# Small vectors through GpSimd's queue, and another order of loads and row work in a kernel of pooled attention and a token-mixing MLP

## The chip, the cores and the metric

The kernel runs on one core of a Trainium2 chip. Its time is that of one launch, in microseconds on the device; the runs of a kernel are given with their median. The core has five engines that run their own instruction streams: TensorE (PE; its weight loads are counted apart as PEld), VectorE (DVE), ScalarE (ACT), GpSimd (POOL) and SyncE (SP), which here only issues transfers. Sixteen DMA engines carry the transfers of all queues.

## The reference

Eight batches, eight heads of 64, 576 tokens. The keys and values are averaged over groups of eight tokens, so each head has 72 of them. The attention's output is the input of one token-mixing MLP layer.

```python
k_p = k.reshape(B, H, 72, 8, D).mean(axis=3)
v_p = v.reshape(B, H, 72, 8, D).mean(axis=3)
scores = scale * np.matmul(q, k_p.transpose(0, 1, 3, 2))
attn = softmax(scores)
x = np.matmul(attn, v_p)          # as (B, 576, 512)
a1 = alpha1 * x + beta1
u = x + lam * np.einsum('ts,bsd->btd', w_tok, a1)
a2 = alpha2 * u + beta2
out = u + lam * (np.maximum(a2 @ w_ch1, 0.0) @ w_ch2)
```

## The kernel before, in words

**Tiles.** A batch's q and k come as two tiles `qk_raw` (four heads each, tokens 0 to 511, f32, 512 KB for q and 512 KB for k) and one small tile `rem_raw` (tokens 512 to 575, four transfers of 64 KB). v comes as two tiles `v_u`, each by two transfers: 64 groups and the last 8. The tiles of each kind have two buffers, so a new load waits until its buffer's readers are done.

**Attention of one batch.** GpSimd casts q to `q_bf` (L112) and sums k over four tokens into `k_bf` (L119, L120), and does the same for the remainder (L105, L106); batch 0 has VectorE or ScalarE do some of it. TensorE transposes q (`att_F`), finishes the pooling of k with a matrix of eighths (`att_K`, casts to `kpT` at L334), and VectorE sums v over eight tokens (`att_V`, L340 and L342, into `vp`). Then, head by head, `att_S` makes the scores and their exponentials (ScalarE, L354), `att_AV` the weighted sums with a column for the denominator, a reciprocal and a product on VectorE (L374, L376) into `x_tm`, and after every second head `att_X` scales two heads' columns into the bf16 tile `xs` (L383, the four full row tiles, and L387, the remainder).

**Mix and MLP.** `mix_T` multiplies `w_tok` with `xs` for one row tile (five matmuls of 512 columns, L417), adds `x` on VectorE (L419) and scales to `u_bf` (L421). `mix_uT` transposes `u_bf` into `u_fm`. The MLP takes blocks of four row tiles, 9 blocks for the 36 row tiles of all batches: sixteen first-layer tiles `mlp_A` (four matmuls of 512 columns, a ReLU on ScalarE at L446) and then sixteen second-layer parts `mlp_B` (four matmuls, L459; the last part of a row tile adds to `u` at L464, and the output transfer goes out at L466).

**What sets the order.** Nothing is scheduled by a tool. The front (L473 to L545) is written out: it does batch 0's attention and mix. For the blocks, `todo` holds pairs of a position and a step, and they are issued in order of the position: first-layer tiles at 0 to 15, second-layer parts at 16 to 31, the next batch's attention and mix among them (block n does batch n + 1), and the loads of the batch after that. Each engine runs its own instructions in the order in which they were issued. In block 0, batch 1's work stands later (`late`), since its loads come late. `keep_warm` gives TensorE matmuls on zeros that nobody reads.

**Queues.** SyncE issues all loads of q, k, v and all outputs; ScalarE's queue issues five loads of small vectors (alpha1, lam, alpha2, beta1, beta2) at the start; GpSimd's queue issues `w_tok` and the eight weight loads, which cast from f32 to bf16 on the way. SyncE's and ScalarE's transfers take eight completion semaphores in turn, so the ninth transfer waits until the first has landed, and so on. GpSimd's queue has eight of its own.

## Time and profile before

| | |
|---|---|
| median of 3 runs | 395.27 us (394.63 to 396.18) |
| the profiled execution | 391.7 us, span of its instructions 390.0 us |
| TensorE busy | 360.9 us (93% of the span) |
| VectorE, ScalarE, GpSimd busy | 226.3, 189.9 and 72.1 us |
| mean granted TensorE clock | 0.992 |
| bytes moved | 43.01 MB, 110 GB/s over the span |

The profile is one execution with the start and the duration of each instruction. A matmul's duration includes its way through the array, so four matmuls in a row take less than four durations; rows that stand for several (x4) give the time from the first start to the last end. What an engine waited for stands in brackets behind its row, with the idle time.

### The profile page before, as it was taken

The page shows a single profiled execution, that of the slowest core. Times are in us where ns is not written, and L with a number is a line of the kernel's source. Part 1 is how long each engine was busy: PE and PEld are TensorE (multiplying, and loading weights), DVE is VectorE, ACT ScalarE, POOL GpSimd, SP SyncE. Part 2 cuts the span into 40 slices and gives each one's busy share as a digit, 9 for nine tenths or more (in the row PEclk, how much of TensorE's full clock was granted, in tenths as well). Part 3 has the DMA queues.
Part 4 walks back from the last instruction along what each step waited for, and adds up shares of the span by engine and source line. Part 5 has one row for each costly group of instructions (what it writes and reads, how often), then busy time and mean ns, then how long its engine had stood idle before and what let it go on. Part 6 is the DMA issues. An engine that isn't in the chain of part 4 may idle for free.

```text
span 390.0 us, 5932 instructions
## 1 busy us (share of the span) xinstructions
PE 360.9 (93%) x2275; PEld 193.8 (50%) x2275; DVE 226.3 (58%) x469; ACT 189.9 (49%) x380; POOL 72.1 (18%) x86
## 2 busy tenths in 40 slices
PE   6579999699999999899989998999899999999994
PEld 2355555345554555355535553455455544544541
DVE  6677459875497549745875578637873685011011
ACT  3644666117831683168505860387038713822710
POOL 6272243420150015000510042003300000000000
PEclk9999999989999999999999999999999999999998
DMA  5999995903861187116811591139210011002011
GB/s 176 246 166 214 258 196 111 229 31 106 203 162 55 55 202 162 55 54 140 224 55 50 119 251 44 42 84 249 82 44 12 2 55 55 0 27 82 0 53 57
DMA packets 34705, 43.01 MB, mean 110 GB/s; under 512 B 2218, under 2 KB 24814, under 8 KB 34676
## 3 DMA queue, kind: packets, MB, share of 16 engines
q1 hardware_dynamic: 31744, 37.76, 37.7%
q0 software_dynamic: 2912, 4.86, 7.0%
q8 instruction: 18, 0.29, 0.3%
q14 instruction: 11, 0.09, 0.1%
q10 hardware_dynamic: 20, 0.01, 0.0%
HBM read 38.04 MB, written 9.44 MB: 122 GB/s over the span
## 4 chain that ended last, share of the span: by engine, by line
PE 73%; DVE 19%; DMA 4%; issue 1%; ACT 1%; SPq 1%; POOL 1%
PE ps_h L443 32%; PE ps_ch L459 21%; PE ps_tok L417 12%; DVE x_tm L376 5%; DVE xs L383 5%; DMA qk_raw<-in_k_dram 4%; DVE xs L387 3%; PE ps_uT L432 2%; PE ps_sc L352 2%; DVE rec L374 2%; DVE u_sb L464 2%; PE ps_q L298 1%; PE ps_av L368 1%; PE ps_warm L407 1%; DVE v_u L340 1%
## 5 line engine op out<-in xcount | busy, mean ns | idle before, releaser
L459 PE MATMUL ps_ch<-w,Hj 128*128 128x512 bf16 x576 | 141.4, 381 | 0.0
L443 PE MATMUL ps_h<-u_fm,w 128*128 128x512 bf16 x576 | 132.4, 379 | 0.0
L446 ACT ACTIVATE Hj<-ps_h,bias_cols 128x512 bf16<-128x512 f32 x144 | 99.1, 689 | 40.4 <-PE ps_h L443 39.3
L443 PEld LDWEIGHTS <-w 128*128 128x128 bf16 x576 | 62.9, 114 | 49.8 <-issue 0.3
L459 PEld LDWEIGHTS <-Hj 128*128 128x128 bf16 x576 | 54.6, 98 | 50.9 <-issue 2.2
L434 ACT COPY u_fm<-ps_uT 128x512 bf16<-128x512 bf16 x36 | 21.1, 586 | 101.2 <-PE ps_uT L432 101.0
L417 PE MATMUL ps_tok<-xs,wtT 128*128 128x512 bf16 (+1 forms) x200 | 50.7, 385 | 10.7 <-DVE xs L383 10.7
L354 ACT ACTIVATE ET<-ps_sc 72x288 f16<-72x288 f32 x128 | 44.8, 402 | 26.7 <-PE ps_sc L352 25.9
L464 DVE TENSOR_TENSOR u_sb<-u_sb,ps_ch 128x512 f32<-128x512 f32 x36 | 24.4, 681 | 50.3 <-PE ps_ch L459 50.2
L419 DVE TENSOR_TENSOR u_sb<-x_tm,ps_tok 128x512 f32<-128x512 f32 (+1 forms) x40 | 27.5, 687 | 35.4 <-PE ps_tok L417 35.1
L340 DVE TENSOR_TENSOR v_u<-v_u 72x512 f32<-72x512 f32 x64 | 36.4, 569 | 3.2 <-DMA v_u<-in_v_dram 1.7
L417 PEld LDWEIGHTS <-wtT 128*128 128x128 bf16 (+1 forms) x200 | 18.8, 99 | 35.0 <-DVE xs L383 13.9
L334 DVE CAST kpT<-ps_kp 64x144 bf16<-64x144 f32 x32 | 9.8, 305 | 43.1 <-PE ps_kp L330 42.9
L376 DVE TENSOR_TENSOR x_tm<-ps_av,rec 128x320 f32<-128x320 f32 x64 | 31.5, 492 | 2.2
L112 POOL CAST q_bf<-qk_raw 128x1024 bf16<-128x1024 f32 x14 | 14.9, 1065 | 87.0 <-DMA qk_raw<-in_q_dram 87.0
L352 PE MATMUL ps_sc<-qT,kpT 128*72 128x288 bf16 x128 | 28.3, 307 | 2.1 <-DVE x_tm L376 1.1
L421 DVE TENSOR_TENSOR u_bf<-u_sb,al_bc 128x512 bf16<-128x512 f32 (+1 forms) x38 | 26.7, 702 | 1.5
L119 POOL TENSOR_TENSOR qk_raw<-qk_raw 128x512 f32<-128x512 f32 x16 | 22.2, 1387 | 19.8 <-DMA qk_raw<-in_k_dram 16.8
L383 DVE TENSOR_TENSOR xs<-x_tm,lamal_bc 128x512 bf16<-128x512 f32 x31 | 25.1, 808 | 1.0
L368 PEld LDWEIGHTS <-ET 72*128 72x128 f16 x256 | 16.7, 102 | 17.5 <-DVE vp L342 2.5
L374 DVE RECIPROCAL rec<-ps_av 128x5 f32<-128x5 f32 x64 | 12.1, 189 | 17.4 <-PE ps_av L372 16.9
L368 PE MATMUL ps_av<-vp,ET 72*128 72x66 f16 x256 | 18.7, 199 | 3.6 <-DVE vp L342 3.6
(91 smaller groups left out, 236.6 us busy)
## 6 DMA issues: line engine op xcount, KB each, us to landing
qk_raw<-in_q_dram SPq DMA_DIRECT2D x16, 512.0 KB, 8.0
qk_raw<-in_k_dram SPq DMA_DIRECT2D x16, 512.0 KB, 7.6
v_u<-in_v_dram SPq DMA_DIRECT2D x16, 512.0 KB, 5.6
out_dram<-u_sb SPq DMA_DIRECT2D x32, 256.0 KB, 3.4
w<-in_moe_w_ch_dram POOLq DMA_DIRECT2D x8, 512.0 KB, 12.5
rem_raw<-in_q_dram SPq DMA_DIRECT2D x16, 64.0 KB
rem_raw<-in_k_dram SPq DMA_DIRECT2D x16, 64.0 KB, 2.3
v_u<-in_v_dram SPq DMA_DIRECT2D x16, 64.0 KB
```

The costliest lines, as they stand in the source:

```text
L340: nc.vector.tensor_tensor(out=t[:, :, 0:n], in0=t[:, :, 0:n], in1=t[:, :, n:2 * n], op=ALU.add)
L352: nc.tensor.matmul(out=ps_sc[0:SPG, 0:288], lhsT=kpT_pool[u][:, hh, r, :], rhs=st["qT"][u][:, S * r + n0:S * r + n0 + 288])
L354: nc.scalar.activation(out=ET[:, 64 + n0:64 + n0 + 288], in_=ps_sc[0:SPG, 0:288], func=AF.Exp, bias=0.0, scale=0.125)
L368: nc.tensor.matmul(out=av[:, c, :], lhsT=ET[:, m0:m0 + 128], rhs=vp1[:, hh, :])
L376: nc.vector.tensor_tensor(out=x[:, :, dd:dd + D], in0=av[:, :, 0:64], in1=rec.unsqueeze(2).to_broadcast((P, 5, D)), op=ALU.mult)
L383: eng.tensor_tensor(out=xs[:, 0:4, cols], in0=x[:, 0:4, cols], in1=lamal_bc[:, cols].unsqueeze(1).to_broadcast((P, 4, D * (h1 - h0))), op= ...
L417: nc.tensor.matmul(out=ps_tok, lhsT=wtT[0:kk, at, t0:t0 + P], rhs=xs[0:kk, sc, :], start=(sc == 0), stop=(sc == 4))
L419: nc.vector.tensor_tensor(out=s["u"][p0:p1, :], in0=st1[b]["x"][p0:p1, c, :], in1=ps_tok[p0:p1, 0:DM], op=ALU.add)
L443: nc.tensor.matmul(out=ps_h, lhsT=w1_of(cc, j), rhs=u_fm[n][:, cc, :], start=(cc == 0), stop=(cc == 3))
L446: nc.scalar.activation(out=t, in_=ps_h, func=AF.Relu, bias=bias_cols[:, j:j + 1], scale=1.0)
L459: nc.tensor.matmul(out=ps, lhsT=Hj[n, j][:, 128 * m:128 * m + 128], rhs=w2[j // 4][:, j % 4, :], start=(j == 0), stop=(j == NJ - 1))
L464: nc.vector.tensor_tensor(out=u, in0=u, in1=ps, op=ALU.add)
```

## The change

**Loads at the start.** The five small vectors go through GpSimd's queue, two ahead of its mask building and three behind it. On SyncE's queue the first v tile stands ahead of the remainder, and the v tile's small part behind it. `load_v` takes a list of the parts that it issues. beta1 times lam is multiplied straight into `xs`, where it went through a tile `lamb1` and two copies.

**The front.** The `kpT` casts of batch 0 are ScalarE's (`att_K` with `nc.scalar.copy`). The third broadcast (alpha2) and the transposed beta2 stand behind the first four heads' scores. Both v sums of the second half stand ahead of its scores. The scaling of two heads that GpSimd does stands earlier, the first row sum of `w_tok` behind the last weighted sums, and of the 13 matmuls of `keep_warm` 5 stay. The four mixes follow each other, and the first four first-layer tiles begin on three of the four row tiles (384 columns) before the last row tile is transposed; the last 128 columns follow.

**The blocks.** The q and k loads of the batch after the next move to positions 0.4 and 1.4, the remainder to 0.9, and v to 5.8 and 12.4 (before: remainder 3.5, v 4.6 and 11.2, q and k right behind each). `q_bf` and `k_bf` get a fourth buffer. Scores, weighted sums and mixes of batches 2 to 7 stand one position earlier. In block 0 the first two of four `att_X` are GpSimd's, and the four scalings of `w2` (L276) stand at 4.2 to 9.3, before at 5.0 to 14.0.

SyncE's queue at the start of the program, before. The names are the tile and the input tensor; `DMAHW0` to `DMAHW7` are the completion semaphores that an issue waits for.

```order
L77 DMA qk_raw<-in_q_dram 128x4x256
L77 DMA qk_raw<-in_k_dram 128x4x256
L87 DMA rem_raw<-in_q_dram 128x1x128 x2
L87 DMA rem_raw<-in_k_dram 128x1x128 [waits DMAHW0_49]
L87 DMA rem_raw<-in_k_dram 128x1x128 [waits DMAHW1_49]
L96 DMA v_u<-in_v_dram 64x4x512 [waits DMAHW3_49]
L96 DMA v_u<-in_v_dram 8x4x512 [waits DMAHW4_49]
L77 DMA qk_raw<-in_q_dram 128x4x256 [waits DMAHW5_49]
L77 DMA qk_raw<-in_k_dram 128x4x256 [waits DMAHW6_49]
```

The same place after:

```order
L77 DMA qk_raw<-in_q_dram 128x4x256
L77 DMA qk_raw<-in_k_dram 128x4x256
L99 DMA v_u<-in_v_dram 64x4x512
L87 DMA rem_raw<-in_q_dram 128x1x128 x2
L87 DMA rem_raw<-in_k_dram 128x1x128 x2
L99 DMA v_u<-in_v_dram 8x4x512
L77 DMA qk_raw<-in_q_dram 128x4x256 [waits DMAHW0_49]
L77 DMA qk_raw<-in_k_dram 128x4x256 [waits DMAHW1_49]
```

Eight transfers now stand ahead of the first wait, where four stood, and v's large part is the third.

VectorE in the front, from the last product of the first four heads to the sums of the second v tile, before:

```order
L376 TENSOR_TENSOR x_tm_252<-ps_av_280,rec_286 128x5x64
L334 CAST kpT_1_139<-ps_kp_316 64x144 x2
L383 TENSOR_TENSOR xs_0_157<-x_tm_252,lamal_bc_72 128x4x128
L387 TENSOR_TENSOR xs_0_157<-x_tm_252,lamal_bc_72 64x128
L383 TENSOR_TENSOR xs_0_157<-x_tm_252,lamal_bc_72 128x4x128
L387 TENSOR_TENSOR xs_0_157<-x_tm_252,lamal_bc_72 64x128
L340 TENSOR_TENSOR v_u_102<-v_u_102 72x2x256
L340 TENSOR_TENSOR v_u_102<-v_u_102 72x2x128
L342 TENSOR_TENSOR vp1_2_144<-v_u_102 72x2x64
```

The same place after:

```order
L380 TENSOR_TENSOR x_tm_249<-ps_av_277,rec_283 128x5x64
L387 TENSOR_TENSOR xs_0_155<-x_tm_249,lamal_bc_72 128x4x128
L391 TENSOR_TENSOR xs_0_155<-x_tm_249,lamal_bc_72 64x128
L387 TENSOR_TENSOR xs_0_155<-x_tm_249,lamal_bc_72 128x4x128
L391 TENSOR_TENSOR xs_0_155<-x_tm_249,lamal_bc_72 64x128
L344 TENSOR_TENSOR v_u_95<-v_u_95 72x2x256
L344 TENSOR_TENSOR v_u_95<-v_u_95 72x2x128
L346 TENSOR_TENSOR vp1_2_142<-v_u_95 72x2x64
```

The two casts of `kpT`, for which VectorE had to wait until the second k had been summed, no longer stand ahead of the slices and the v sums.

SyncE's queue from the last output of a block into the next block, before:

```order
L466 DMA out_0_dram<-u_sb_1089 128x512 [waits DMAHW4_49,DVE_49]
L87 DMA rem_raw_1669<-in_q_dram 128x1x128 [waits DMAHW5_49]
L87 DMA rem_raw_1669<-in_q_dram 128x1x128 [waits DMAHW6_49]
L87 DMA rem_raw_1669<-in_k_dram 128x1x128 [waits DMAHW7_49]
L87 DMA rem_raw_1669<-in_k_dram 128x1x128 [waits DMAHW0_49]
L96 DMA v_u_1681<-in_v_dram 64x4x512 [waits DMAHW1_49,DVE_49]
L96 DMA v_u_1681<-in_v_dram 8x4x512 [waits DMAHW2_49]
L77 DMA qk_raw_1684<-in_q_dram 128x4x256 [waits DMAHW3_49,Pool_49]
L77 DMA qk_raw_1684<-in_k_dram 128x4x256 [waits DMAHW4_49]
L96 DMA v_u_1770<-in_v_dram 64x4x512 [waits DMAHW5_49,DVE_49]
```

The same place after:

```order
L477 DMA out_0_dram<-u_sb_1091 128x512 [waits DMAHW7_49,DVE_49]
L77 DMA qk_raw_1640<-in_q_dram 128x4x256 [waits DMAHW0_49,Pool_49]
L77 DMA qk_raw_1640<-in_k_dram 128x4x256 [waits DMAHW1_49]
L87 DMA rem_raw_1643<-in_q_dram 128x1x128 [waits DMAHW2_49]
L87 DMA rem_raw_1643<-in_q_dram 128x1x128 [waits DMAHW3_49]
L87 DMA rem_raw_1643<-in_k_dram 128x1x128 [waits DMAHW4_49]
L87 DMA rem_raw_1643<-in_k_dram 128x1x128 [waits DMAHW5_49]
L77 DMA qk_raw_1655<-in_q_dram 128x4x256 [waits DMAHW6_49,Pool_49]
L77 DMA qk_raw_1655<-in_k_dram 128x4x256 [waits DMAHW7_49]
L99 DMA v_u_1720<-in_v_dram 64x4x512 [waits DMAHW0_49,DVE_49]
```

Both q, k pairs now stand right behind the output, and no v load, with its wait for VectorE, stands ahead of them.

The diff, cut to its core:

```diff
-        bf = work.tile([P, 4, 4, D], BF, tag="q_bf", bufs=3, name="q_bf")
+        bf = work.tile([P, 4, 4, D], BF, tag="q_bf", bufs=4, name="q_bf")
...
     load_qk(0, 0)
-    for i, src in ((1, moe_alpha1), (0, moe_lam), (2, moe_alpha2), (3, moe_beta1)):
-        n = 65 if i in (0, 3) else 1
-        nc.scalar.dma_start(out=vecs[0:n:64, i],
-                            in_=src.unsqueeze(0).to_broadcast((1 + n // 65, DM)))
-    nc.scalar.dma_start(out=b2row, in_=moe_beta2.rearrange("(c p) -> c p", p=P))
+    load_v(0, 0, (0,))
     load_rem(0)
-    load_v(0, 0)
+    load_v(0, 0, (1,))
     load_qk(0, 1)
     load_v(0, 1)
+    for i, src in ((1, moe_alpha1), (0, moe_lam)):
+        n = 65 if i in (0, 3) else 1
+        nc.gpsimd.dma_start(out=vecs[0:n:64, i],
+                            in_=src.unsqueeze(0).to_broadcast((1 + n // 65, DM)))
...
+    nc.gpsimd.dma_start(out=vecs[0:65:64, 3], in_=moe_beta1.unsqueeze(0).to_broadcast((2, DM)))
+    nc.gpsimd.dma_start(out=vecs[0:1, 2], in_=moe_alpha2.unsqueeze(0))
+    nc.gpsimd.dma_start(out=b2row, in_=moe_beta2.rearrange("(c p) -> c p", p=P))
...
-    def mlp_A(n, j):
-        ps_h = gp("ps_h")
+    def mlp_A(n, j, t0=0, t1=512):
+        if t0 == 0:
+            ps_A[j] = gp("ps_h")
+        ps_h = ps_A[j]
         for cc in range(4):
-            nc.tensor.matmul(out=ps_h, lhsT=w1_of(cc, j), rhs=u_fm[n][:, cc, :],
+            nc.tensor.matmul(out=ps_h[:, t0:t1], lhsT=w1_of(cc, j), rhs=u_fm[n][:, cc, t0:t1],
                              start=(cc == 0), stop=(cc == 3))
...
-    broadcast(2, al2_bc)
-    setup_vectors()
...
-    att_K(0, 0, nc.vector.tensor_copy)
+    att_K(0, 0, nc.scalar.copy)
     for h in range(4):
         att_S(0, h)
...
     att_V(0, 1)
+    broadcast(2, al2_bc)
+    setup_vectors()
     for h in range(4):
         att_AV(0, h)
...
-    att_K(0, 1, nc.vector.tensor_copy)
+    att_K(0, 1, nc.scalar.copy)
     att_X(0, 0, 2)
     att_X(0, 2, 4)
     att_V(0, 2)
+    att_V(0, 3)
     for h in (4, 5, 6):
         att_S(0, h)
-    att_V(0, 3)
...
     setup_wtok(0, nc.scalar.copy)
+    att_X(0, 4, 6, nc.gpsimd)
     setup_wtok(1, nc.scalar.copy)
-    keep_warm(3)
-    att_X(0, 4, 6, nc.gpsimd)
-    setup_rowsum(0)
     att_AV(0, 6)
     att_AV(0, 7)
+    setup_rowsum(0)
     setup_wtok(2, nc.scalar.copy)
     setup_rowsum(1)
-    keep_warm(3)
+    setup_wtok(3, nc.scalar.copy)
     att_X(0, 6, 8)
...
     mix_uT((0, 2))
-    keep_warm(2)
+    keep_warm(3)
+    mlp_A(0, 0, 0, 384)
     mix_uT((0, 3))
-    keep_warm(3)
+    for j in range(1, 4):
+        mlp_A(0, j, 0, 384)
+    for j in range(4):
+        mlp_A(0, j, 384, 512)
...
-            at = 17.0 + 0.9 * h if late else 14.1 + 1.0 * h
+            at = 17.0 + 0.9 * h if late else 13.1 + 1.0 * h
...
-                todo.append((at + lag + 0.1, lambda h=h: att_X(b, h - 1, h + 1)))
+                eng = nc.gpsimd if late and h < 5 else nc.vector
+                todo.append((at + lag + 0.1, lambda h=h, eng=eng: att_X(b, h - 1, h + 1, eng)))
         for c in range(5):
-            at = 26.2 + 0.9 * c if late else 26.0 + c
+            at = 26.2 + 0.9 * c if late else 25.0 + c
...
-                todo.append((5.0 + 3 * g, lambda g=g: scale_w2(g)))
+                todo.append((4.2 + 1.7 * g, lambda g=g: scale_w2(g)))
...
-                late = 17.0 if b == 1 else 0.0
-                todo.append((late + 3.5, lambda b=b: load_rem(b + 1)))
                 for u in range(2):
-                    at = 22.0 + 0.1 * u if b == 1 else 4.6 + 6.6 * u
+                    at = 20.0 + 0.2 * u if b == 1 else 0.4 + 1.0 * u
+                    todo.append((at, lambda b=b, u=u: load_qk(b + 1, u)))
+                    at = 22.0 + 0.2 * u if b == 1 else 5.8 + 6.6 * u
                     todo.append((at, lambda b=b, u=u: load_v(b + 1, u)))
-                    todo.append((at + 0.1, lambda b=b, u=u: load_qk(b + 1, u)))
+                todo.append((20.1 if b == 1 else 0.9, lambda b=b: load_rem(b + 1)))
```

More of the change, by code (lines that the diff above doesn't have):

```diff
@@ L90, in load_rem, with load_v @@
         st1[b]["rem_raw"] = raw
-    def load_v(b, u):
-        v_u = work.tile([SPG, 4, 8, D], FP, tag="v_u", bufs=2, name="v_u")
-        for g0, g1 in ((0, 64), (64, SPG)):
+    def load_v(b, u, parts=(0, 1)):
+        if parts[0] == 0:
+            st1[b]["v"][u] = work.tile([SPG, 4, 8, D], FP, tag="v_u", bufs=2, name="v_u")
+        v_u = st1[b]["v"][u]
+        for part in parts:
+            g0, g1 = ((0, 64), (64, SPG))[part]
             nc.sync.dma_start(
@@ L98, in load_v @@
                 in_=v[b, 4 * u:4 * u + 4, 8 * g0:8 * g1].rearrange("h (g p) d -> g h (p d)", p=8))
-        st1[b]["v"][u] = v_u
     def cast_rem(b, eng, copy=None):
@@ L117, in sum_k @@
         raw = st1[b]["raw"][u][:, 1]
-        bf = work.tile([P, 4, D], BF, tag="k_bf", bufs=3, name="k_bf")
+        bf = work.tile([P, 4, D], BF, tag="k_bf", bufs=4, name="k_bf")
         eng.tensor_tensor(out=raw[:, :, 0:2], in0=raw[:, :, 0:2], in1=raw[:, :, 2:4], op=ALU.add)
@@ L581 @@
         todo = []
-        for j in range(NJ):
+        for j in range(0 if n else 4, NJ):
             todo.append((j, lambda j=j: mlp_A(n, j)))
```

24 lines of the change are left out of this document (12 added, 12 removed).

## The prediction

> **What bounds the kernel now.** I read the table of busy time by stretches first, cut where the work changes its kind: the front up to the first token mix, the mix and the first four first-layer tiles, the end of block 0, and then one row for each block. Columns: stretch, length, busy us of PE, PEld, DVE, ACT and POOL (instructions), the granted clock, the share of the DMA engines, GB/s.
>
> ```profile
> 0.00:30.48 30.48, 20.28 (x124) 12.25 (x125) 21.06 (x70) 15.37 (x36) 15.52 (x28) 1.00 0.91 196
> 30.48:42.10 11.62, 11.59 (x90) 6.63 (x91) 8.99 (x11) 5.60 (x11) 2.54 (x2) 1.00 1.10 216
> ...
> 73.00:76.38 3.38, 0.02 (x1) 0.00 (x0) 3.20 (x8) 0.00 (x0) 1.05 (x1) 1.00 1.12 246
> 76.38:80.89 4.51, 4.51 (x14) 1.72 (x15) 1.65 (x3) 0.00 (x0) 3.51 (x3) 0.62 0.14 40
> ...
> 88.85:128.63 39.78, 38.73 (x255) 21.06 (x252) 25.92 (x55) 21.16 (x43) 7.52 (x8) 1.00 0.47 123
> 128.63:169.69 41.06, 38.88 (x254) 21.02 (x253) 27.49 (x56) 20.56 (x42) 7.84 (x8) 1.00 0.44 113
> 169.69:209.67 39.98, 38.51 (x251) 20.87 (x249) 25.79 (x54) 21.16 (x43) 7.56 (x8) 1.00 0.44 116
> 209.67:250.72 41.05, 38.89 (x255) 20.97 (x253) 27.48 (x56) 20.64 (x42) 7.23 (x8) 1.00 0.46 113
> 250.72:290.30 39.58, 38.51 (x251) 20.87 (x249) 25.39 (x54) 21.15 (x43) 6.99 (x8) 1.00 0.45 117
> 290.30:329.64 39.34, 38.89 (x255) 21.00 (x253) 25.77 (x56) 20.57 (x42) 0.00 (x0) 1.00 0.09 28
> ```
>
> TensorE is the bound nearly everywhere. What can be won is where it stands: 10.2 us of the front, 3.4 us ahead of batch 1's mix with 4.5 us at clock 0.62 behind it, and 0.5 to 2.2 us in each of six blocks. Next I read the list of waits:
>
> ```profile
> PE ps_tok L417 <- DVE xs L383: 10.7, 7, 3.4
> ...
> PE ps_uT L432 <- DVE u_bf L421: 1.3, 3, 0.4
> ```
>
> The mix stands for the last scaled slice `xs`, so VectorE ends last there. GpSimd's column says more: the one block without GpSimd work, the last row, has the smallest gap. The timeline of the second block shows why; start and duration stand ahead.
>
> ```profile
> 152.79 1.26 POOL L119 TENSOR_TENSOR qk_raw<-qk_raw 128x512 f32<-128x512 f32 x1 [0.27 <-PE ps_av L372]
> 153.04 1.56 DVE L383 TENSOR_TENSOR xs<-x_tm,lamal_bc 128x512 bf16<-128x512 f32 x1
> 154.13 1.05 POOL L120 TENSOR_TENSOR k_bf<-qk_raw 128x256 bf16<-128x256 f32 x1
> ...
> L383 DVE TENSOR_TENSOR xs<-x_tm,lamal_bc x31: 677/693/1715, 20.7 to 317.3; 128x512 bf16<-128x512 f32 x31
> ```
>
> Beside GpSimd's two k sums the slice takes 1.56 us; its median is 0.69.
>
> **The change, steady blocks.** The next batch's q and k loads move to positions 0.4 and 1.4 of a block, the remainder between them, v behind them (5.8, 12.4). Before, the second half came so late that GpSimd summed its k at 152.79, 24 us into its block, among the slices. The way from issue to cast, and the first slice, in the block that starts at 88.85:
>
> ```profile
> 98.37 0.40 SPq L77 DMA_DIRECT2D qk_raw<-in_q_dram  x1
> ...
> 105.02 1.04 POOL L112 CAST q_bf<-qk_raw 128x1024 bf16<-128x1024 f32 x1 [10.15 <-DMA qk_raw<-in_q_dram]
> ...
> 107.64 0.79 DVE L383 TENSOR_TENSOR xs<-x_tm,lamal_bc 128x512 bf16<-128x512 f32 x1
> ```
>
> Eight issues of some half a microsecond behind the last output put the second q about 5 us into the block; 6.65 us to its cast and 1.04 + 1.26 + 1.05 for cast and sums: GpSimd is done 15 to 16 us in. The first slice comes at 18.8, and 1.3 us earlier since attention moves one position up: 17.5. The overlap goes with about 2 us to spare. Mix and attention move together, so three second-layer parts still cover the stretch from the last head to the mix; one residual add (row tile 1) falls behind the last slice and gives VectorE 0.6 us more. The `ps_tok` waits are the gaps of the five rows from 88.85, less 0.42 (a third of 1.3) that two of them lose at `ps_uT`: 1.05 + 1.76 + 1.47 + 1.74 + 1.07 = 7.1 us. The `ps_uT` waits stay; the fifth mix and its transpose keep their order. What is late next is ScalarE, with three heads' exponentials beside first-layer tiles in place of two, and the v sums beside GpSimd's casts: I leave 0.5 us. **Gain 6.6 us**, bounds 1.0 (the casts still collide) and 7.1.
>
> **Block 0.**
>
> ```profile
> 56.31 2.28 DVE L276 TENSOR_TENSOR w<-w,lam_bc 128x2048 bf16<-128x2048 bf16 x1
> ...
> 69.15 0.69 DVE L383 TENSOR_TENSOR xs<-x_tm,lamal_bc 128x512 bf16<-128x512 f32 x1
> ...
> 69.86 1.03 DVE L387 TENSOR_TENSOR xs<-x_tm,lamal_bc 64x128 bf16<-64x128 f32 x1
> ...
> 76.38 1.98 PE L417 MATMUL ps_tok<-xs,wtT 128*128 128x512 bf16 x5 [3.37 <-DVE xs L383]
> ```
>
> VectorE is the chain up to this mix (3.20 of the 3.38 us). The last `w2` scaling, 2.28, leaves it for a stretch in which VectorE idles; it is hidden there as long as its weights have landed. Two slice pairs go to GpSimd: 1.72 by the rows, and at least 0.69 for the other. That is 4.7 us. On GpSimd a pair takes 1.26 us (its slice in the front, quoted below) and its remainder; it is ready before the last slice, but may hold VectorE up by 1.56 - 0.69 = 0.87 each time. I take half, 0.9 in all: 3.8 us, more than the wait of 3.37. Then TensorE doesn't stand and the clock stays: 4.51 us at 0.62 are 2.8 at full rate, 1.7 saved. 3.4 + 1.7, less 0.4 for what may remain: **gain 4.7 us**, bounds 2.5 (part of the wait stays) and 6.0 (small stalls before it go too).
>
> **The front.**
>
> ```profile
> SPq L77 <- DMA qk_raw<-in_q_dram: 2.4, 1, 2.4
> ...
> 5.00:10.00 5.00, 4.59 (x13) 2.16 (x13) 2.83 (x4) 1.71 (x4) 3.63 (x5) 1.00 0.57 161
> ...
> 6.37 3.78 PE L215 MATMUL ps_bc<-vecs,ones_row 1*128 1x512 f32 x4
> ...
> 11.07 2.36 PE L352 MATMUL ps_sc<-qT,kpT 128*72 128x288 bf16 x8 [0.47 <-DVE kpT L334]
> ...
> 14.58 0.40 PE L368 MATMUL ps_av<-vp,ET 72*128 72x66 f16 x4 [1.15 <-DVE vp L342]
> ...
> 17.42 0.49 DVE L376 TENSOR_TENSOR x_tm<-ps_av,rec 128x320 f32<-128x320 f32 x1
> ...
> 18.05 0.49 DVE L376 TENSOR_TENSOR x_tm<-ps_av,rec 128x320 f32<-128x320 f32 x1
> ...
> 20.75 0.69 DVE L383 TENSOR_TENSOR xs<-x_tm,lamal_bc 128x512 bf16<-128x512 f32 x1
> ...
> 23.87 0.38 PE L368 MATMUL ps_av<-vp,ET 72*128 72x66 f16 x4 [1.79 <-DVE vp L342]
> ...
> 25.93 1.48 PE L407 MATMUL ps_warm<-warm,identity_bf 128*128 128x512 bf16 x3
> ...
> 26.67 1.26 POOL L383 TENSOR_TENSOR xs<-x_tm,lamal_bc 128x512 bf16<-128x512 f32 x1 [1.87 <-DVE x_tm L376]
> ...
> 30.48 1.24 PE L417 MATMUL ps_tok<-xs,wtT 128*128 128x512 bf16 x5 [0.20 <-DVE xs L383]
> ```
>
> SyncE's issues wait for completions (2.4 us for one q load) while the DMA engines are 0.57 busy. ScalarE's five small loads leave the lanes and the order changes, so eight transfers go out at once: v and the second k land earlier. The first weighted sum (14.58) gains nothing from it. The scores can start at some 10.3 in place of 11.07, once the remainder is in, and take 2.36; one of the two broadcasts in the row at 6.37 (3.78 / 2 = 1.9) now stands behind them: 14.7. From there VectorE is the chain. Four reciprocals and products at 0.63 (18.05 - 17.42) end at 17.6, before at 18.54; the kpT casts are ScalarE's now, so two slice pairs of 0.97 follow at once, not at 20.75, and end at 19.5; the next v pair is summed by 20.95 (two adds and a third, 2 x 0.57 + 0.29):
>
> ```profile
> L340 DVE TENSOR_TENSOR v_u<-v_u 72x512 f32<-72x512 f32 x64 | 36.4, 569 | 3.2 <-DMA v_u<-in_v_dram 1.7
> L342 DVE TENSOR_TENSOR vp<-v_u 72x128 f16<-72x128 f32 x32 | 9.3, 291 | 1.1
> ```
>
> So the sum of 23.87 starts at 21.0. From there to the mix it took 6.61 us; six warming matmuls go, three at half rate and three later ones (1.3 and 0.6 us), which leaves 4.7, and 0.2 for transposes that run at half rate longer: the mix starts at 25.9 instead of 30.48, 4.6 earlier. The stretch behind it, 11.62 us, stays about as long: two of its seven warming matmuls go (0.4), and four first-layer tiles come in pieces of 384 and 128 columns, with the same columns in all but sixteen more weight loads, of which I leave 0.5 us unhidden. **Gain 4.5 us**, bounds 2.0 and 6.5.
>
> [...]
>
> **The sum.** 6.6 + 4.7 + 4.5 = 15.8 us. The profiled execution took 391.7 us (span 390.0 and 1.7 around it) and would take 375.9. The runs' median, 395.27, lies 3.57 above it; the same gain from there gives **379.5 us**. With each term halfway to its bounds the forecast's own range is 376 to 384.
>
> **Rivals.**
>
> *GpSimd still collides (0.17).* For it: GpSimd takes its casts in order, the remainder first, so one late 64 KB load holds all of them; and batch 2's casts now queue behind GpSimd's slices at the end of block 0. Against it: the 2 us above. Steady gain 1.0, block 0 its wait of 3.4 without the clock, front 4.5: 8.9 us, 386.4.
>
> *The vectors come late (0.08).* The first broadcast heads TensorE's queue, and alpha now comes through GpSimd's queue. From ScalarE's it was issued at 0.94, and the broadcast began at 2.39; in GpSimd's the quickest landing is that of a 512 KB weight load, 5.4 us:
>
> ```profile
> 0.94 0.52 ACTq L150 DMA_DIRECT2D vecs<-in_moe_alpha_dram  x1
> 2.39 2.04 PE L215 MATMUL ps_bc<-vecs,ones_row 1*128 1x512 f32 x2 [2.39 <-DMA vecs<-in_moe_alpha_dram]
> ...
> DMA to landing us min/median/max: 5.4/12.5/19.6
> ```
>
> Between 2.4 and 0.9 + 5.4 = 6.3 I take 3.5, nearer the small load's; up to there the first q cast hides it. At 6.3 the scores start 2.1 us later than in the sum: front 2.4, 381.6. [...]
>
> *Half clock in the front (0.06).* If a gap stays between the weighted sums and the mix, the stretch of 11.62 us runs at 0.62: 18.7, 7.1 longer, 386.6.
>
> *Slower (0.03).* GpSimd's casts, moved to where VectorE sums v, delay those sums until the weighted sums stand for them long enough for the clock to fall. By the rows at 73.00 and 76.38 that is 3.4 + 1.7 = 5.1 us in each of six blocks, 30.6, less 7.1, 4.7 and 4.5: 14.3 slower, 409.6. It decides from 16.3 / 6 = 2.7 us a block. Against it: VectorE is busy only 25 to 27 of 40 us.
>
> **Chances.** Forecast 0.60, the rivals 0.34, several of them together, up to no change, 0.06. The range reaches over all rivals but the slower one and takes in the forecast's own: 375.0 to 387.5; out of it lie the slower case, the several, and the outer ends of the forecast and of GpSimd's collision, some 0.2 together. About 0.5% is what a measurement can tell from no change here. Faster 0.94, same 0.03, slower 0.03.
>
> **What would show it.** Right: the mix starts near 25.9; no `ps_tok` wait above 0.5 us; clock 1.00 behind batch 1's mix; GpSimd done by 16 us into a block and all slices near 0.69 us. Wrong: a first broadcast after 4 us, GpSimd beside the slices, or waits for `vp` in the blocks.

## The result, and the profile after

The changed kernel takes **378.69 us** (median of 4 runs, 377.85 to 379.3), the kernel before beside it 394.95 us (4 runs, 393.52 to 396.18): a ratio of 0.9588 with a 95% interval of 0.9548 to 0.9628, 16.3 us less. The forecast was 379.5 us. The profiled execution took 379.15 us, with a span of 377.4; against the profiled execution of before (391.7, span 390.0) that is 12.6 us.

First the table of busy time by stretches, cut as before. Columns: stretch, length, busy us of PE, PEld, DVE, ACT, POOL (instructions), granted clock, share of the DMA engines, GB/s.

```profile
0.00:29.38 29.38, 18.14 (x117) 11.48 (x118) 21.13 (x67) 15.22 (x38) 18.17 (x32) 1.00 1.06 205
29.38:40.60 11.22, 11.19 (x104) 7.28 (x105) 8.50 (x11) 4.05 (x9) 2.54 (x2) 1.00 1.09 215
40.60:72.45 31.85, 28.69 (x242) 16.39 (x238) 21.62 (x41) 19.66 (x45) 15.29 (x17) 1.00 0.97 223
72.45:76.05 3.60, 3.60 (x9) 1.31 (x10) 1.83 (x3) 0.00 (x0) 3.52 (x4) 0.53 0.02 5
...
84.97:123.31 38.34, 38.34 (x253) 20.92 (x250) 26.51 (x55) 20.95 (x43) 7.37 (x8) 1.00 0.43 128
123.31:162.44 39.13, 38.71 (x254) 21.11 (x253) 27.18 (x54) 20.96 (x43) 7.73 (x8) 1.00 0.43 119
...
317.37:377.40 60.03, 55.42 (x257) 26.98 (x255) 6.20 (x9) 22.02 (x32) 0.00 (x0) 0.99 0.11 40
```

The steady blocks stand nearly without a gap now: 38.34 of 38.34 us, and 38.71 of 39.13 where the 0.42 at `ps_uT` is left. Behind batch 1's mix the clock is still halved (0.53 over 3.60 us). The front is hardly shorter, 29.38 against 30.48. Cut at the first first-layer tile of a block, the 12.6 us are made up so:

| stretch | before | after | gained | forecast |
|---|---|---|---|---|
| front, to the fourth first-layer tile | 42.10 | 40.60 | 1.5 | 4.5 |
| the rest of block 0 | 46.81 | 44.37 | 2.4 | 4.7 |
| six blocks, 1 to 6 | 240.57 | 232.40 | 8.2 | 6.6 |
| the end | 60.52 | 60.03 | 0.5 | 0 |
| span | 390.0 | 377.4 | 12.6 | 15.8 |

The list of waits of TensorE says the same. The line of 10.7 us for the slice `xs` in seven waits is down to two, both ahead of the steady blocks, and the wait for alpha1, 2.4 us before, heads the list:

```profile
PE ps_bc L219 <- DMA vecs<-in_moe_alpha_dram: 7.2, 1, 7.2
PE ps_tok L421 <- DVE xs L387: 2.6, 2, 2.0
...
PE ps_uT L436 <- DVE u_bf L425: 1.3, 3, 0.4
```

The timeline of the front, start and duration ahead, shows why it gained so little:

```profile
1.37 0.71 POOL L157 DMA_DIRECT2D vecs<-in_moe_alpha_dram  x1 [0.47 <-issue]
...
7.21 2.04 PE L219 MATMUL ps_bc<-vecs,ones_row 1*128 1x512 f32 x2 [7.21 <-DMA vecs<-in_moe_alpha_dram]
...
11.45 1.54 DVE L492 TENSOR_TENSOR xs<-vecs 1x512 bf16<-1x512 f32 x2 [6.07 <-DMA vecs<-in_moe_beta_dram]
11.69 0.76 POOL L108 TENSOR_TENSOR rem_k<-rem_raw 128x128 bf16<-128x128 f32 x1 [2.76 <-DMA rem_raw<-in_k_dram]
...
14.13 2.14 PE L356 MATMUL ps_sc<-qT,kpT 128*72 128x288 bf16 x8 [0.36 <-ACT kpT L338]
```

alpha1 is there 5.84 us after its issue, beta1 only at 11.45, and the remainder, now issued behind 512 KB of v, at 11.69. Three late transfers stand ahead of scores that began at 11.07 before.

In block 0, batch 2's casts (POOL) follow GpSimd's own two slices, and lie on VectorE's last slice:

```profile
70.58 1.26 POOL L121 TENSOR_TENSOR qk_raw<-qk_raw 128x512 f32<-128x512 f32 x1
70.74 1.65 DVE L387 TENSOR_TENSOR xs<-x_tm,lamal_bc 128x512 bf16<-128x512 f32 x1
71.92 1.05 POOL L122 TENSOR_TENSOR k_bf<-qk_raw 128x256 bf16<-128x256 f32 x1
72.42 0.70 DVE L391 TENSOR_TENSOR xs<-x_tm,lamal_bc 64x128 bf16<-64x128 f32 x1
72.45 2.31 PE L421 MATMUL ps_tok<-xs,wtT 128*128 128x512 bf16 x5 [2.04 <-DVE xs L387]
```

In the first steady block, which starts at 84.97, GpSimd's last sum ends at 101.4, 16.4 us in, and the first slice comes 1.6 us later and takes its 0.69:

```profile
100.63 0.79 POOL L122 TENSOR_TENSOR k_bf<-qk_raw 128x256 bf16<-128x256 f32 x1
103.05 0.69 DVE L387 TENSOR_TENSOR xs<-x_tm,lamal_bc 128x512 bf16<-128x512 f32 x1
```

### The profile page after: what moved, and what is told of

Its sections match the earlier page's. It is cut to its first block, busy times and chain, and to the rows that moved or that the text cites. A ratio compares the mean times of both kernels' runs of the same rounds, so it can differ in the third digit from the quotient of the medians.

```text
span 377.4 us, 5931 instructions
## 1 busy us (share of the span) xinstructions
PE 357.1 (95%) x2283; PEld 194.3 (51%) x2283; DVE 228.4 (61%) x462; ACT 187.8 (50%) x382; POOL 78.0 (21%) x94
## 4 chain that ended last, share of the span: by engine, by line
PE 87%; DVE 8%; DMA 2%; issue 1%; POOL 1%; ACT 0%; POOLq 0%; DVEq 0%
PE ps_h L452 33%; PE ps_ch L470 31%; PE ps_tok L421 12%; PE ps_sc L356 4%; PE ps_uT L436 2%; DMA vecs<-in_moe_beta_dram 2%; PE ps_av L372 2%; PE ps_q L302 2%; DVE x_tm L380 2%; DVE v_u L344 2%; DVE xs L387 1%; DVE vp L346 1%; DVE u_sb L423 1%; DVE u_bf L425 1%; PE ps_bias L290 1%
## 5 line engine op out<-in xcount | busy, mean ns | idle before, releaser
L452 PE MATMUL ps_h<-u_fm,w 128*128 128x512 bf16 (+2 forms) x592 | 133.6, 373 | 0.0
L452 PEld LDWEIGHTS <-w 128*128 128x128 bf16 x592 | 64.0, 114 | 48.6 <-issue 0.3
L344 DVE TENSOR_TENSOR v_u<-v_u 72x512 f32<-72x512 f32 x64 | 43.2, 674 | 2.6 <-DMA v_u<-in_v_dram 1.1
L107 POOL CAST rem_q<-rem_raw 128x256 bf16<-128x256 f32 x7 | 3.7, 528 | 140.6 <-PE ps_h L452 92.5
L421 PEld LDWEIGHTS <-wtT 128*128 128x128 bf16 (+1 forms) x200 | 19.4, 99 | 25.9 <-DVE xs L387 2.5
L338 DVE CAST kpT<-ps_kp 64x144 bf16<-64x144 f32 x28 | 8.5, 305 | 38.4 <-PE ps_kp L334 38.2
L121 POOL TENSOR_TENSOR qk_raw<-qk_raw 128x512 f32<-128x512 f32 x16 | 23.0, 1437 | 5.4 <-DMA qk_raw<-in_k_dram 5.4
L387 DVE TENSOR_TENSOR xs<-x_tm,lamal_bc 128x512 bf16<-128x512 f32 x29 | 21.4, 739 | 0.9
L114 POOL CAST q_bf<-qk_raw 128x1024 bf16<-128x1024 f32 x14 | 16.4, 1175 | 13.9 <-DMA qk_raw<-in_q_dram 13.9
```

Source lines behind the costliest of these rows:

```text
L344: nc.vector.tensor_tensor(out=t[:, :, 0:n], in0=t[:, :, 0:n], in1=t[:, :, n:2 * n], op=ALU.add)
L387: eng.tensor_tensor(out=xs[:, 0:4, cols], in0=x[:, 0:4, cols], in1=lamal_bc[:, cols].unsqueeze(1).to_broadcast((P, 4, D * (h1 - h0))), op= ...
L421: nc.tensor.matmul(out=ps_tok, lhsT=wtT[0:kk, at, t0:t0 + P], rhs=xs[0:kk, sc, :], start=(sc == 0), stop=(sc == 4))
L452: nc.tensor.matmul(out=ps_h[:, t0:t1], lhsT=w1_of(cc, j), rhs=u_fm[n][:, cc, t0:t1], start=(cc == 0), stop=(cc == 3))
```

## The experiments

All start from the changed kernel. "Mix" is the start of batch 0's first mix, "block 1" its first first-layer tile, "six blocks" the time from there to the same tile of block 7, all of the profiled execution. The kernel before had medians of 392.87, 393.07, 393.43 and 394.29 beside the four groups of runs.

| run | median us (runs) | mix | block 1 | six blocks |
|---|---|---|---|---|
| the change | 378.69 (4) | 29.38 | 84.97 | 232.40 |
| f1_vecs_scalar | 377.94 (4) | 28.85 | 83.03 | 232.40 |
| f2_rem_first | 376.14 (4) | 27.62 | 83.01 | 232.40 |
| f3_both | 377.94 (4) | 27.94 | 83.99 | 232.40 |
| f4_data_later | 384.73 (1) | 31.68 | | |
| b1_casts_late | 377.70 (4) | 29.47 | 83.98 | 232.40 |
| b2_all_vector | 381.24 (4) | 29.39 | 88.85 | 232.41 |
| s1_loads_back | 385.25 (4) | 29.38 | 84.78 | 239.07 |
| s2_heads_back | 377.87 (4) | 29.41 | 83.11 | 232.99 |
| d1_broadcast_later | 375.41 (4) | 26.86 | 83.95 | 232.40 |
| e1_third_pair | 376.86 (5) | 29.44 | 87.74 | 232.41 |
| m1_whole_tiles | 379.56 (4) | 29.64 | 83.96 | 232.40 |
| c2_front_third | 375.24 (6) | 28.32 | 82.28 | 232.40 |

Two things in this table are chance. Block 1's time contains the clock behind batch 1's mix, which costs 1.69 us in some executions and nothing in others (last section): the change and s2 have the same mix, to 0.03 us, and block 1 at 84.97 and 83.11. And in block 0 VectorE waits for v in some executions, for up to 4.10 us. So medians that lie some tenths apart (f1, f3, s2 and b1; c2 and d1) are not told apart. The mix isn't the end of the front either: the first first-layer tile of block 0 starts at 36.73 in the change, 36.69 in f1, 34.97 in f2, 35.30 in f3, 34.64 in d1 and 35.69 in c2.

### The front: four runs

The first edit (f1) takes alpha1, lam and beta1 to ScalarE's queue, ahead of all other loads in the program; the second (f2) puts the remainder ahead of v; f3 does both.

```diff
+    for i, src in ((1, moe_alpha1), (0, moe_lam), (3, moe_beta1)):
+        ...
+        nc.scalar.dma_start(out=vecs[0:n:64, i], ...)
     new_batch(0)
     load_qk(0, 0)
```

```diff
-    load_v(0, 0, (0,))
     load_rem(0)
-    load_v(0, 0, (1,))
+    load_v(0, 0)
```

**f1.** 

> The changed kernel with alpha1, lam and beta1 loaded first of all through ScalarE's queue; all else as changed. Theory (two delays stand one behind the other in the front, the vectors through GpSimd's queue and the remainder behind 512 KB of v, and each alone is enough): first broadcast at 2.4 instead of 7.21, but the remainder still lands at about 11.5, so the first scores start at 13.2 instead of 14.13 and the mix at 28.4 instead of 29.38; about 377.7 us. Rival (the vectors alone are the delay): scores at 10.5, mix near 26, 375.3 us.

**f2.** 

> The changed kernel with the remainder's four loads ahead of v in SyncE's queue; vectors through GpSimd's queue as changed. Theory (two delays, each enough): the remainder lands near 8, but beta1 still at about 11.4 and its product stands ahead of the remainder's cast on VectorE, so scores stay at 14.1 and the mix within 0.5 us of 29.38; about 378.7 us. Rival (the remainder alone is the delay): scores at 11 or earlier, mix near 26.5, 375.8 us.

**f3.** 

> Both edits together: vectors first through ScalarE's queue, and the remainder ahead of v. Theory: both delays gone, scores at 10.5 and mix at 26 to 26.5, three us earlier than in the changed kernel; about 375.5 us. Rival (the front is bound by something behind the scores, v's landing or VectorE's sums): scores earlier but the mix within 1 us of 29.38; 378 us.

The run f1 was nearer to my theory than to its rival, with each step later than I had written: broadcast at 3.57 (2.4 expected), remainder at 12.55 (11.5), scores at 13.62 (13.2), mix at 28.85 (28.4). I had overlooked that only alpha1 is early in it. lam, issued through ScalarE's queue at 1.49, is waited for until 7.72, and beta1, issued at 2.12, until 11.00, where it was 11.45 through GpSimd's queue:

```profile
7.72 2.07 PE L218 MATMUL ps_bc<-vecs,ones_row 1*128 1x512 f32 x2 [0.96 <-DMA vecs<-in_moe_lam_dram]
...
11.00 1.39 DVE L491 TENSOR_TENSOR xs<-vecs 1x512 bf16<-1x512 f32 x2 [5.33 <-DMA vecs<-in_moe_beta_dram]
```

So the queue is not what made them late. Nor do the 0.53 us at the mix reach the first-layer tiles (36.69 against 36.73): f1's mix began slower, with five matmuls in 1.74 us for 1.24 (last section).

The run f2 did not go as my theory had it: its scores came earlier, and the time fell by more than in f1. From its timeline:

```profile
8.26 0.45 POOL L108 TENSOR_TENSOR rem_k<-rem_raw 128x128 bf16<-128x128 f32 x1
8.27 1.70 DVE L491 TENSOR_TENSOR xs<-vecs 1x512 bf16<-1x512 f32 x2 [2.88 <-DMA vecs<-in_moe_beta_dram]
9.46 2.07 PE L218 MATMUL ps_bc<-vecs,ones_row 1*128 1x512 f32 x2
...
12.38 2.13 PE L355 MATMUL ps_sc<-qT,kpT 128*72 128x288 bf16 x8 [0.40 <-ACT kpT L337]
```

beta1, through the same queue at the same time, is there at 8.27 instead of 11.45. So the two delays aren't independent, as I had put it: with v issued ahead, at 1.84, the vectors wait behind it as well, through either queue, as beta1 in f1 shows. What is left is lam's broadcast, which holds TensorE from 9.46 to 11.5 ahead of the remainder's transposes. The run f3 has its scores at 10.20 (10.5 expected) and its first weighted sums at 14.27, but not the mix at 26 to 26.5:

```profile
10.20 2.13 PE L354 MATMUL ps_sc<-qT,kpT 128*72 128x288 bf16 x8 [0.36 <-ACT kpT L336]
12.05 1.14 DVE L342 TENSOR_TENSOR v_u<-v_u 72x512 f32<-72x512 f32 x2 [1.92 <-DMA v_u<-in_v_dram]
...
21.39 1.14 DVE L342 TENSOR_TENSOR v_u<-v_u 72x512 f32<-72x512 f32 x2 [1.56 <-DMA v_u<-in_v_dram]
...
27.94 1.24 PE L419 MATMUL ps_tok<-xs,wtT 128*128 128x512 bf16 x5 [0.26 <-DVE xs L385]
```

Now the second half of v is late (and that of k, for which TensorE stood 1.88 us). With ScalarE's three loads back among them, SyncE issued the second q at 7.45, against 5.77 in f2. From the first weighted sums to the mix it took 13.67 us, where the change (18.20 to 29.38), f1 and f2 took 11.16 to 11.18. The rival of f3 was the better description.

f4 asks what delays alpha1: all loads of batch 0's data wait until VectorE's fills are done.

```diff
-    load_qk(0, 0)
     ...
+    load_qk(0, 0, nc.vector)     # behind the fills
```

**f4.** 

> Diagnosis of alpha's late landing: the changed kernel with all loads of batch 0's q, k, v and remainder held behind VectorE's first fills (start near 4.7 us instead of 0.81), the vectors through GpSimd's queue as changed. Theory traffic (alpha's descriptors and packets stand in line with 512 KB transfers): alpha, issued at 1.4, lands by 3.9 while the fills still run, so the first broadcast starts by 4. [...] Total a few us longer than 379, since the data come 3.9 us later.

```profile
1.37 0.71 POOL L150 DMA_DIRECT2D vecs<-in_moe_alpha_dram  x1 [0.48 <-issue]
...
3.37 2.04 PE L219 MATMUL ps_bc<-vecs,ones_row 1*128 1x512 f32 x2 [3.37 <-DMA vecs<-in_moe_alpha_dram]
```

The issue stands at the same 1.37, VectorE's fills run from 0.94 to 4.69 as they did, and alpha1 is there after 2.00 us instead of 5.84. So it is the data's traffic that delays it, and not the fills, which run beside it here as well.

### Block 0: two runs, and the third pair

b1 loads batch 2's q, k and remainder later, b2 gives VectorE all four slice pairs, e1 gives GpSimd three.

```diff
-    at = 20.0 + 0.2 * u if b == 1 else 0.4 + 1.0 * u
+    at = 25.0 + 0.2 * u if b == 1 else 0.4 + 1.0 * u       # b1; the remainder at 25.1
...
-    eng = nc.gpsimd if late and h < 5 else nc.vector
+    eng = nc.vector                                        # b2
+    eng = nc.gpsimd if late and h < 6 else nc.vector       # e1
```

**b1.** 

> The changed kernel with batch 2's q, k and remainder loaded later in block 0 (positions 25.0 to 25.2 instead of 20.0 to 20.2, so behind v), so that GpSimd's casts of them begin behind the last slice. Theory (batch 2's casts, queued right behind GpSimd's two slices, hold VectorE's last slice up): the slice of 1.65 us takes 0.69, batch 1's first mix waits at most 0.6 instead of 2.04 and starts near 71, the clock stays at full rate behind it, block 1 starts near 82.5 instead of 85.1; about 376.2 us. Rival (VectorE's chain is late by itself, by its wait of 1.08 for v and the sums ahead): mix within 0.5 of 72.45, the half clock stays; 378.7 us. Third (the casts now stand beside the mix's adds): wait gone but given back, 378 to 379.

**b2.** 

> The changed kernel with all four slice pairs of block 0 on VectorE, as before the change; loads as changed. Theory (the two pairs on GpSimd win little, since they push batch 2's casts onto VectorE's last slice): VectorE has 1.9 us more to do but GpSimd is done with the casts before the last slice, so the first mix of batch 1 starts within 0.8 us of 72.45; about 379 us. Rival (the offload is worth its full 1.9 us and more): mix at 74.4 or later, 380.7 us or more.

**e1.** 

> The changed kernel with three of block 0's four slice pairs on GpSimd instead of two; loads as changed, so batch 2's casts queue behind the third pair. Theory (VectorE's tail is the chain into batch 1's mix, and batch 2's casts hold its last slice up): the last slice starts near 70.0 and takes 0.7 to 1.0, the mix starts near 71.1 instead of 72.45 after a wait of at most 0.7, the clock stays at full rate, block 1 starts near 82.2 instead of 85.0; 376 us. Rival (GpSimd's third pair holds VectorE up as the casts did, or is itself late): mix at 72 or later, 378.5 us or more.

In b1 the last slice takes 0.69, the mix waits 0.98 and the clock stays at 1.00. But the casts now lie beside the mix's own products, and part of the gain goes back: from the mix to block 1 it takes 12.11 us, where 10.84 is the shortest that any run shows. The third reading was the nearest.

```profile
71.87 1.25 PE L421 MATMUL ps_tok<-xs,wtT 128*128 128x512 bf16 x5 [0.98 <-DVE xs L387]
...
75.69 1.04 POOL L114 CAST q_bf<-qk_raw 128x1024 bf16<-128x1024 f32 x1
75.83 1.45 DVE L425 TENSOR_TENSOR u_bf<-u_sb,al_bc 128x512 bf16<-128x512 f32 x1
```

b2 went against my theory: 381.24 us, 2.55 more than the change, so the offload of two pairs is worth about what the rival said. Its profiled execution alone would overstate this (mix of batch 1 at 76.33), since VectorE waited 2.77 us for v there; the four runs, 380.05 to 382.96, all lie above the change's, but how much of the 2.55 us is v's landing in the other three isn't shown.

e1's profiled execution lost 4.10 us to a late v (the first row below), and the clock with it (0.50 over the 5.4 us from 64.75 on), and so says nothing on the total; but the mix behind it shows the mechanism: the last slice is short, the wait 0.29 us, and the clock 1.00 over the next 3.6 us. The other four runs took 376.52 to 377.18. That the saved time is there is shown; that it is smaller than the 2.7 us that I expected fits the casts beside the products (11.67 us from mix to block 1), but no run tests that.

```profile
62.48 1.14 DVE L344 TENSOR_TENSOR v_u<-v_u 72x512 f32<-72x512 f32 x2 [4.10 <-DMA v_u<-in_v_dram]
...
75.32 0.69 DVE L387 TENSOR_TENSOR xs<-x_tm,lamal_bc 128x512 bf16<-128x512 f32 x1
...
76.07 1.25 PE L421 MATMUL ps_tok<-xs,wtT 128*128 128x512 bf16 x5 [0.29 <-DVE xs L387]
```

### The steady blocks: loads or positions

```diff
-    at = 20.0 + 0.2 * u if b == 1 else 0.4 + 1.0 * u        # q, k
+    at = 20.0 + 0.2 * u if b == 1 else 4.7 + 6.6 * u        # s1; v and remainder back too
...
-    at = 17.0 + 0.9 * h if late else 13.1 + 1.0 * h
+    at = 17.0 + 0.9 * h if late else 14.1 + 1.0 * h         # s2; the mix back at 26.0 too
```

**s1.** 

> The changed kernel with the loads of the steady blocks at their old positions (remainder 3.5, v 4.6 and 11.2, q and k 4.7 and 11.3). Theory (the loads are the steady gain): GpSimd's k sums stand beside the slices again, slices of about 1.56 us, waits for the slice ahead of five mixes of 1.0 to 1.8 us; the blocks from 85.14 to 317.54 take 238.5 to 240 us instead of 232.4; about 385.7 us. Rival (heads and mix one position earlier are the gain): 233 to 234.5 us, 379.5 to 381.

**s2.** 

> The changed kernel with the heads and the mix of the steady blocks back at positions 14.1 and 26.0; loads as changed. Theory (the loads alone carry the gain): no wait for a slice above 0.5 us, six blocks within 1.2 us of 232.4; about 378.9 us. Rival (the earlier position carries 2 us or more of the 8.4): the blocks take 234.5 us or more, 381 us or more.

With the old loads GpSimd's sum stands on a slice again, and the waits are back:

```profile
147.89 1.27 POOL L121 TENSOR_TENSOR qk_raw<-qk_raw 128x512 f32<-128x512 f32 x1 [0.39 <-DMA qk_raw<-in_k_dram]
148.02 1.69 DVE L387 TENSOR_TENSOR xs<-x_tm,lamal_bc 128x512 bf16<-128x512 f32 x1
...
152.60 0.60 PE L421 MATMUL ps_tok<-xs,wtT 128*128 128x512 bf16 x2 [1.48 <-DVE xs L387]
```

The loads carry 239.07 - 232.40 = 6.7 of the 8.2 us, the positions 0.6; the other 0.9 belongs to neither alone (with the old loads the rest of the change gains 1.5, with the old positions 7.6). Both went as my theory had it, but for s2's total, 1.0 us under the one expected.

### The first tiles in pieces

```diff
-    mlp_A(0, 0, 0, 384)
     mix_uT((0, 3))
-    for j in range(1, 4):
-        mlp_A(0, j, 0, 384)
     for j in range(4):
-        mlp_A(0, j, 384, 512)
+        mlp_A(0, j)
```

**m1.** 

> The changed kernel with block 0's first four first-layer tiles whole, behind the transposes of all four chunks, instead of 384 and then 128 columns each. Theory (TensorE then stands for the copy of the fourth chunk, which ends at 38.40, while the pieces start at 36.73): the bias matmuls behind the four tiles start near 41.8 instead of 40.45; 380 us. Rival (the pieces cost what they save, by sixteen more weight loads): 40.4 to 40.8, 378.7 us.

TensorE stands 0.67 us for the fourth row tile's copy, and the bias matmuls behind the four tiles start 11.67 us after the mix, against 11.07 in the change: the pieces win 0.6, half of what I expected, since without them the fourth transpose came earlier (36.80 instead of 37.38).

```profile
36.80 0.39 PE L436 MATMUL ps_uT<-identity_bf,u_bf 128*128 128x128 bf16 x4
37.86 3.62 PE L452 MATMUL ps_h<-u_fm,w 128*128 128x512 bf16 x16 [0.67 <-ACT u_fm L438]
41.31 0.67 PE L290 MATMUL ps_bias<-b2c_bf,w 128*128 128x1 bf16 x16
```

### Two versions made of what was found

d1 has the remainder ahead of v, the vectors where the change has them, and an order in which nothing heads a queue that waits for a vector; c2 adds the third pair of e1 and puts alpha2's broadcast behind the weighted sums.

```diff
-    broadcast(1, lamal_bc)
     cast_q(0, 0, nc.vector.tensor_copy)
     att_F(0, 0)
     att_F(0, 1)
-    broadcast(0, lam_bc)
+    broadcast(1, lamal_bc)
     sum_k(0, 0, nc.gpsimd)
+    cast_rem(0, nc.gpsimd, nc.vector.tensor_copy)
+    att_Frem(0, (0,), nc.vector.tensor_copy)
+    att_K(0, 0, nc.scalar.copy)
     ...                          # beta1 * lam into xs
-    cast_rem(0, nc.gpsimd, nc.vector.tensor_copy)
-    att_Frem(0, (0,), nc.vector.tensor_copy)
-    att_K(0, 0, nc.scalar.copy)
     for h in range(4):
         att_S(0, h)
-    nc.vector.tensor_tensor(out=lamal_bc, in0=lamal_bc, in1=lam_bc, op=ALU.mult)
+    broadcast(0, lam_bc)
     ...
+    nc.gpsimd.tensor_tensor(out=lamal_bc, in0=lamal_bc, in1=lam_bc, op=ALU.mult)
-    broadcast(2, al2_bc)         # c2 only: to behind att_AV(0, 0..3)
-    setup_vectors()
```

**d1.** 

> The kernel with the remainder ahead of v, and TensorE's queue in an order in which nothing stands behind the vectors: q's transposes ahead of alpha1's broadcast, lam's broadcast behind the first four heads' scores, the beta1 product behind the remainder's cast and K; the lam product of the first vector on GpSimd. The vectors stay on GpSimd's queue. Theory (the front is late by what queues behind the vectors and by the remainder; from the first weighted sum on it takes 11.2 us to the mix): scores near 10 instead of 12.38, weighted sums at 14.1 to 14.5 instead of 16.45, mix at 25.6 to 26.6 instead of 27.62; 374 to 375 us. Rival (the second half of k and v lands too late, as where it was waited for at 21.39): weighted sums early, but mix at 27.3 or later, 376 us.

**c2.** 

> What the runs point to, in one kernel: the remainder ahead of v; q's transposes ahead of alpha1's broadcast, lam's broadcast behind the first scores, alpha2's broadcast and the beta2 transpose behind the first four weighted sums (they stood ahead of them where the sums began at 15.13); three of block 0's slice pairs on GpSimd. Theory (the front's late start and VectorE's tail in block 0 are two separate losses, so the gains add): weighted sums from 14.2, mix at 26 to 26.9, batch 1's first mix after a wait of at most 0.7, clock at full rate behind it; 373.5 to 374.5 us. Rival (in block 0 v lands no earlier, so what the front wins is waited for there): block 1 starts no earlier than 83.0, 375 us or more.

d1's scores start at 9.35, but I had overlooked that alpha2's broadcast still stood ahead of the weighted sums: two broadcasts take 3.78, and the sums start at 15.13. The mix comes at 26.86, 0.3 later than the theory's end, and the median is 375.41 us.

```profile
9.35 2.14 PE L355 MATMUL ps_sc<-qT,kpT 128*72 128x288 bf16 x8 [0.37 <-ACT kpT L337]
...
11.42 3.78 PE L218 MATMUL ps_bc<-vecs,ones_row 1*128 1x512 f32 x4
...
15.13 0.40 PE L371 MATMUL ps_av<-vp,ET 72*128 72x66 f16 x4
...
58.58 1.14 DVE L343 TENSOR_TENSOR v_u<-v_u 72x512 f32<-72x512 f32 x2 [3.20 <-DMA v_u<-in_v_dram]
```

Of the 2.52 us that d1's mix is ahead of the change's, 1.03 are left at batch 1's mix (71.42 against 72.45): VectorE waits 3.20 us for v there (the last row), where the change waits 1.08.

c2 does in block 0 what it should (wait 0.44, clock 1.00, block 1 at 82.28, the earliest of all), but its front is worse than d1's: alpha2's copy stands ahead of the second q cast on ScalarE and waits there 4.31 us for TensorE, so the cast starts at 18.92 instead of 15.77, and the mix at 28.32. At 375.24 us (ratio 0.9520, interval 0.9479 to 0.9561) it has the lowest median here, and beats the kernel before; d1's 375.41 can't be told from it, and against the change (0.9548 to 0.9628) the intervals just overlap. Its theory held for the slices of block 0 and not for the front, and the time missed it. The rival was partly right: VectorE waited 2.94 us for v in block 0, and the time is over 375 us, though block 1 starts before 83.0. d1's front with c2's slices wasn't tried.

```profile
18.38 0.59 ACT L220 COPY al_bc<-ps_bc 128x512 f32<-128x512 f32 x1 [4.31 <-PE ps_vec L226]
...
18.92 1.06 ACT L114 CAST q_bf<-qk_raw 128x1024 bf16<-128x1024 f32 x1
```

## Why the prediction was right in total, and where its steps failed

The total is right within 0.8 us, and that is mostly luck. All three terms lie outside the bounds that I gave them: the steady blocks above 7.1, the front below 2.0, block 0 just below 2.5. In the two profiled executions from whose rows the sum was made, 12.6 us were gained for 15.8 forecast.

**Steady blocks, 6.6 forecast, 8.2 measured.** The mechanism was right, and s1 shows that the loads are it. The gaps went as worked out (the same rows before and after):

```profile
88.91:329.48 240.57, 232.19 (x1510) 125.62 (x1508) 157.63 (x326) 125.24 (x255) 37.15 (x40) 1.00 0.39 102
```

```profile
84.97:317.37 232.40, 231.13 (x1509) 126.17 (x1507) 161.42 (x325) 124.55 (x256) 38.49 (x40) 1.00 0.37 105
```

TensorE stood 240.57 - 232.19 = 8.38 us in these blocks before and 232.40 - 231.13 = 1.27 after, 7.11 less, for a forecast of 7.1. The 0.5 that I took off for ScalarE and the v sums was not paid (VectorE's v sums did get slower, 674 ns for 569 on average over the program, and in these blocks nobody waited for them). And TensorE's busy time fell by 1.06 us, which I had no term for; in s1, with the waits back, 0.90 of it is back too. Why busy time goes with the waits was not followed further.

**The front, 4.5 forecast, 1.5 measured.** The step that failed is the start: "alpha lands" at about 3.5, scores at 10.3, weighted sums at 14.7. They came at 7.21, 14.13 and 18.20. What follows was right: from the weighted sums to the mix I had 14.7 to 25.9, 11.2 us, and it took 11.18. The steps between agree too: the second half's weighted sums start 6.1 us behind the first half's (6.3 forecast). The 3.5 us are the late start alone. Two assumptions stood behind it, and both fail for the same reason, the traffic of the data. For alpha1 I took a value near the quickest landing of a load that had gone out first; alpha1 landed in 2.00 us with the data's loads held back (f4), and in 5.84 beside them. And that the remainder would be in by 10 was taken over from before, though the change puts 512 KB of v ahead of it; f2 prices that at 1.8 us of the mix. My own list had the late vectors as a rival, at 2.1 us and 8 in 100, with an upper end of 6.3 for alpha1; the trace shows 7.21. And in f3, with both in time, 25.9 did not come either: the second half of v was late next, which the forecast took to land earlier. f3 issues its loads in another order than the change, so that v would have been late there too is not shown. The half-clock rival didn't come: TensorE had a gap of 0.60 us just ahead of the mix, and the mix's first five matmuls took their 1.24 us. But five transposes at 27.46 still took 0.74 us, and 0.44 only at 28.34 (last section).

**Block 0, 4.7 forecast, 2.4 measured.** The step that failed: "Then TensorE doesn't stand and the clock stays". It stood 2.04 us, since the last slice took 1.65 beside batch 2's casts. I had the cause in the text, as half of the rival in which GpSimd collides, and left it out of the sum. Without the casts there (b1) the wait is 0.98, so VectorE's own chain is a part of it; with a third pair on GpSimd 0.29 and 0.44 (e1, c2).

**The sum against the median.** The profiled executions lie 12.6 us apart, the medians 16.3. The profiled execution of before was 3.25 us under its median of 394.95, that of the change 0.46 over its own. I applied the gain to the median, as if the profiled execution were typical; that the sum of the terms came to 15.8 and the medians to 16.3 is luck. The 32 runs of the kernel before beside the experiments have a median of 393.5, and against that the gain is 14.8. The kernel before scatters more: these 32 runs beside the experiments go from 390.43 us at a mean clock of 0.998 to 397.23 at 0.986. That its many stands (times in which TensorE waits), which cost half clock in some executions and not in others (below), make the scatter, and that the change won there too, is argued and not shown.

**What went as written.** No wait for a slice above 0.5 us in the steady blocks, GpSimd done 16 us into a block, slices at 0.69, no wait for `vp` there. The stretch behind the mix took 11.22 us for a forecast of about 11.6. As evidence against the forecast I had named a first broadcast after 4 us, and it was that for the front alone. The rival that ended slower had no support: TensorE never stood in the steady blocks for more than 0.42 us.

## What to carry to other kernels

Here a small load that heads a chain had to be in before the bulk traffic started, whichever queue issued it: alpha1 took 5.84 us beside the data's loads and 2.00 without them (f4), and in f1 ScalarE's queue issued beta1 2.19 us earlier than GpSimd's had, and it was in only 0.45 us earlier, with v's 512 KB issued ahead of it both times. On top of the remainder's place (f2), ordering the engines' work so that nothing stands behind the vectors brought the mix 0.76 us forward (d1), and another queue put it 0.32 back (f3). A front that ends earlier is not yet a kernel that ends earlier: the next load that everything waits for takes its part of the gain (d1). Where one engine is slower beside another (a slice took 1.65 us for 0.69 here), place the one that waits for data by when its data land; here the load's position did it, and the kernel's work stayed as it was. And take the clock's cost of a stand as a chance (1.69 us behind five of eight equal stands), from several executions, not from one profile.
